# A fused attention and mixture kernel: a quarter of one weight's float64 conversion moves to another stage, with narrower postmix products and a new order where the stages meet

## The chip, the cores and the metric

One core of a Trainium2 chip runs the whole program. The metric is the device time of one execution in microseconds (us). Beside the plain runs there is one profiled execution, whose trace gives every instruction's start and duration. TensorE appears as PE (matmuls) and PEld (its weight loads), VectorE as DVE, ScalarE as ACT, GpSimd as POOL; SPq and ACTq are the instruction queues of SyncE and ScalarE where they issue DMAs.

## The reference

Talking-heads attention over 4 batches, 12 heads, 448 positions and head size 64, then a dense two-layer block, then a soft mixture of 8 experts with 4 slots each. The two weights of the dense block arrive as float64.

```python
scores = scale * np.matmul(q, k.transpose(0, 1, 3, 2))
scores = np.einsum('bhij,hg->bgij', scores, w_pre)
attn = softmax(scores)                       # over j, per mixed head
attn = np.einsum('bhij,hg->bgij', attn, w_post)
x = np.matmul(attn, v)                       # -> (1792, 768)
h = x @ moe_w_in                             # (1792, 2048)
x = (h - np.tanh(h)) @ moe_w_out             # (1792, 768)
logits = x @ phi                             # 32 slots
slot_in = softmax(logits, axis=0).T @ x
slot_out = per expert: relu(slot_in @ w1[e]) @ w2[e]
out = softmax(logits, axis=1) @ slot_out
```

## The kernel before, in words

**Attention** (`talking_heads`) works through 16 chunks of up to 120 query rows. A chunk is cut into slots of up to 10 rows, and slots go in pairs, 92 pairs in all. For a pair, `premix` mixes the heads of the scores on PE (`pm`), DVE takes the row maximum (`mx`), `expo` takes the exponential on ACT (`e`), POOL and DVE make the reciprocal sums and scale the postmix weights (`rv`, `wk`), and two pairs later `postmix` multiplies on PE (`tm`): 32 products of a 64-row by 64-column piece of `e` with 60 columns of `wk`. `gather` copies the result to `aT` on ACT, and `values` multiplies it with v (`vx`). Each piece covers only 56 valid columns (`JH`); the other 8 are zeroes or belong to the next piece, and meet zero rows of v. Scores of the next chunk (`sc`), transposes of q and k, and the re-layout DMA `D<-S` (`regroup`, issued four slots ahead) fill the gaps.

**The float64 conversion** runs beside attention. w_in and w_out are cut into 64 pieces of 128 x 384 elements. A piece is loaded (384 KB), goes through `f64_abs` on ACT, `f64_shift` (two instructions), `f64_head` (one) and `f64_tail` (two) on DVE and `f64_sum` on POOL, and is stored to DRAM (192 KB). A planner in `talking_heads` spreads the pieces evenly over the slots (`due = 6 + i * (NS - D_AHEAD - 17) // len(pieces)`) and picks the calmest slot for each step by its own load counts.

**Stage 1** (`moe_and_slots`) multiplies the tokens in four passes (512, 512, 512 and 256 tokens, `PASS`) with 16 column blocks of w_in; one product is a step `t`, 18 matmuls into a PSUM bank `hp`. Both operands are split into a high and a low part, x by `split_x`, a weight block by `split_w`. In pass 0 each step splits the next weight block (`split_w`, ACT and POOL), saves it to DRAM (`save_w`), gates the last product (five DVE instructions, `gate_first` and `gate_last`), transposes the gated block before that (`turn_g`) and two or three half blocks of w_out (`turn_w`); `turn_bank` hands all transposes two PSUM banks in turn, so that the second `wt` of a step reuses the bank of the first, whose copy DVE makes (L914). Steps 5, 9, 13 and 16 also fold w_out with phi (`fold_first`, `fold_last`). Work is hung on the six parts of a product by `on(c, fn)`. Seven buffers of the expert weights (`mem["ex"]`) are handed to the expert loads from step 17 on; until then 0 to 2 hold w_out blocks and their folds, and 3 to 6 are empty.

**Where the stages meet**, `follow()` is a generator: `next(more)` runs it to its next `yield`. Each engine executes its own instructions strictly in the order written, so what stands behind a waiting instruction waits too.

Of the kernel before, what the change touches and what calls it, by code (L numbers as in the profile page):

```python
# [131 lines left out]
def talking_heads(tc, ident, q, k, v, w_pre, w_post, xd, box, follow):  # L132
# [208 lines left out]
    def recip(s):  # L341
        nc.vector.reciprocal(out=ss_t[s], in_=ss_t[s])  # L342
# [10 lines left out]

    def postmix(s):
        es, wks = e_t.pop(s), wk_t.pop(s)
        xs = [ps.tile([128, 2, NR, NH, IH], FP32, tag="t", name="tm", bufs=2) for _ in range(2)]
        for x in range(2):
            for c in range(NR):
                for i in range(2):
                    for z in range(2):  # L360
                        h = slice(64 * i, 64 * i + 64)
                        j = JP * c + JH * z
                        nc.tensor.matmul(  # L363
                            xs[i][64 * z:64 * z + 64, x, c], lhsT=es[x][h, j:j + 64], rhs=wks[x][h],
                            start=True, stop=True)
        tm_t[s] = xs

# [107 lines left out]
        for lo, hi, hf in ((max(2, t0 - D_AHEAD + 1), t0 + 3, 0), (t0 + 4, start[m - 1] - D_AHEAD - 1, 1)):  # L475
            job(calm("pe", lo, hi), q_half, m, hf, act=0.47, dve=0.53, pe=0.4)
    for m in range(NC):
        step = len(chunks[m + 1][3]) // 3 if m + 1 < NC else 1
        for g in range(3):
            lo = start[m + 1] + T_LAG + 1 + g * step  # L480
            job(calm("pe", lo, lo + step - 1), values, m, g, dve=0.41, pe=2.0)
# [45 lines left out]
    et = [lt.tile([128, SEQ + 64 - JH], FP32, tag=f"e{i}", name="e", bufs=1) for i in range(2 * EB)]  # L527
# [3 lines left out]
    warm = ps.tile([128, 128], FP32, tag="t", name="warm", bufs=2)  # L531

    for p in range(3, NP):
        load_k(0, p)
# [33 lines left out]
    jobs = []  # L568
    more = None
    s = 0  # L570
    while s < NS + T_LAG + 3 or jobs or late:
        live = s < NS
        now[0] = s
        box["both"] = s < NS - D_AHEAD
        if s + D_AHEAD < NS:
            regroup(s + D_AHEAD)
        for f, *a in at.get(("load", s), []):
            f(*a)
        if s % 2 == 0:
            if live:  # L580
                premix(s)
            for f in late:
                f()
            late = []
            if 0 <= s - T_LAG < NS:
                postmix(s - T_LAG)
            if live:
                expo(s)
                guard(s)
        else:  # L590
            if s - 1 < NS:
# [30 lines left out]
    for f in late:  # L622
        f()
    late_stack.close()
    box["go"] = True
    for _ in more:
# [3 lines left out]
def moe_and_slots(tc, ident, xd, wi, wo, wo4, wis, consts, w1, w2, out, box):  # L630
# [161 lines left out]
    def load_x(p):  # L792
        n = PASS[p]
        if p == NPASS - 1:
            xbuf[p] = mem["thp"].tile([128, XW], FP32, tag="x0", name="xc")
            dst = xbuf[p][:, KD * n:2 * KD * n]
        else:
            dst = xbuf[p % 2][1][:, :KD * n]
        nc.sync.dma_start(out=dst.rearrange("p (a s) -> p a s", a=KD), in_=xd[p])

    def split_x(b, c):
        h, l = x_of(b, c, 0), x_of(b, c, 1)
        nc.scalar.activation(out=r32(h), in_=l, func=ACTF.Copy)
        nc.vector.tensor_tensor(out=r32(l), in0=l, in1=h, op=ALU.subtract)

    hps, quads, tok = {}, {}, {}

    def product(t, hooks):
        b, f = divmod(t, NF)
        hp = bank(f"h{t % 3}", [128, PASS[b]], "hp")  # L810
        w = unit(t)
        for c in range(KD):
            for fn in hooks.get(c, []):
                fn()
            m, n = divmod(c, KD // 2)
# [78 lines left out]
    def place(b, k):  # L894
# [2 lines left out]
            return quads["C" if k < 2 else "D"][:, k % 2 * n:(k % 2 + 1) * n]  # L897
        return quads["AECDB"[(b * NQ + k) % 5]]

    def load_o(f):  # L900
        if f < NF:
            nc.sync.dma_start(out=mem["wo"][f % NG], in_=wo[f])

    def turn_w(f, hf):
        x = turn_bank([128, KD // 2, 128], "wt")
        for i in range(KD // 2):
            c = hf * (KD // 2) + i
            nc.tensor.transpose(out=x[:, i, :], in_=mem["wo"][f % NG][:, c * 128:(c + 1) * 128], identity=ident)
# [130 lines left out]
    def step(t):  # L1039
# [345 lines left out]
def fused_kernel(  # L1385
# [40 lines left out]
    def side(hf):  # L1426
# [48 lines left out]
```

## Time and profile before

| | |
|---|---|
| runs (3): median, lowest, highest | 909.75, 909.37, 912.9 us |
| profiled execution: time, span of its instructions | 902.81, 901.1 us |
| busy, share of the span: PE, PEld, DVE, ACT, POOL | 92%, 66%, 62%, 64%, 29% |
| mean granted TensorE clock | 0.983 |
| attention; pass 0 of stage 1; expert tail | to about 471 us; 471 to 560 us; from 800 us |

The busy shares are means over stages that have different limits; what bounds a stage is read in that stage. A wait is idle time of an engine, put down to what ended it.

### The profile page before, as it was taken

To read this page: it belongs to the slowest core of one execution; us is meant where nothing else is said; L and a number is where in the kernel's file an instruction comes from. 1 tells how busy PE (TensorE), PEld (TensorE's weight loads), DVE (VectorE), ACT (ScalarE), POOL (GpSimd) and SP (SyncE) were. 2 spreads that over 40 slices of the span, in tenths; PEclk is the share of its full clock that TensorE was granted. 3 is DMA by queue.
4 is the path that set the end of the run, shared out by engine and by line. 5 is a ranking of instruction groups with operands and counts; after the bars stand their busy time and mean duration, and the time that the engine had idled before them with its cause. 6 is when DMAs were issued, how large, how long until landed. Compare 5 with 4: busy or idle time off the path is not lost.

```text
span 901.1 us, 28664 instructions
## 1 busy us (share of the span) xinstructions
PE 828.2 (92%) x11750; PEld 591.0 (66%) x11750; DVE 558.9 (62%) x1185; ACT 574.3 (64%) x1351; POOL 257.9 (29%) x438
## 2 busy tenths in 40 slices
PE   8878999899989899899889999999999989999985
PEld 6546667566666666566577777767776767865543
DVE  4447868678777678687456666557775776730104
ACT  4757888678877788788656766546654666731013
POOL 6344444444445344445203321000000024600000
PEclk9979999999999999999999999999999999999998
DMA  6988788887888878885758977678754445889998
GB/s 133 229 219 231 224 243 254 233 230 222 237 250 225 232 233 235 247 243 176 235 168 290 316 244 249 231 306 334 277 216 157 159 149 167 317 331 422 424 373 305
DMA packets 145910, 224.53 MB, mean 249 GB/s; under 512 B 60852, under 2 KB 127476, under 8 KB 142196
## 3 DMA queue, kind: packets, MB, share of 16 engines
q1 hardware_dynamic: 142432, 209.83, 73.8%
q10 hardware_dynamic: 3348, 12.87, 3.7%
q8 instruction: 93, 1.52, 0.7%
q14 instruction: 37, 0.30, 0.1%
HBM read 147.96 MB, written 36.18 MB: 204 GB/s over the span
## 4 chain that ended last, share of the span: by engine, by line
PE 63%; DMA 19%; ACT 8%; DVE 6%; issue 3%; SPq 1%; POOL 0%; ACTq 0%; POOLq 0%; DVEq 0%
PE hp L818 25%; DMA D<-S 9%; PE pm L320 6%; PE vx L402 5%; PE sc L286 5%; PE tm L363 4%; ACT e L332 3%; DMA ex<-in_moe_w_dram 3%; PE gt L889 3%; DVE mx L324 3%; DMA xd<-xs 2%; PE lgp L939 2%; ACT S L294 2%; PE so L1301 2%; PE sp L1021 1%
## 5 line engine op out<-in xcount | busy, mean ns | idle before, releaser
L332 ACT ACTIVATE e<-pm,mx 128x448 f32<-128x448 f32 x184 | 115.2, 632 | 84.7 <-DVE mx L324 81.0
L363 PEld LDWEIGHTS tm<-wk,e 64*64 64x64 f32 x5888 | 118.5, 137 | 59.7 <-issue 36.9
L818 PE MATMUL hp<-xa,rg 128*128 128x512 f32 x576 | 152.4, 404 | 0.0
L324 DVE TENSOR_REDUCE mx<-pm 128x1 f32<-128x448 f32 x184 | 106.0, 617 | 65.9 <-PE pm L320 65.5
L363 PE MATMUL tm<-wk,e 64*64 64x60 f32 x5888 | 127.3, 223 | 16.0 <-issue 8.9
L320 PE MATMUL pm<-D,wpre 64*64 64x448 f32 (+2 forms) x736 | 118.5, 568 | 16.7 <-DMA D<-S 13.7
L818 PEld LDWEIGHTS hp<-xa,rg 128*128 128x128 f32 x576 | 102.4, 188 | 28.5 <-issue 10.7
L294 ACT ACTIVATE S<-sc 120x448 f32<-120x448 f32 (+1 forms) x186 | 91.4, 551 | 10.5 <-PE sc L286 5.1
L349 POOL TENSOR_SCALAR wk<-wpost,rv 128x60 f32<-128x60 f32 x184 | 89.3, 507 | 16.1 <-DVE rv L342 11.9
L286 PE MATMUL sc<-khi,qT 64*120 64x448 f32 (+1 forms) x384 | 84.6, 392 | 9.6 <-DVE xs L412 7.2
L780 POOL TENSOR_TENSOR rg<-rg 128x384 fp32r<-128x384 f32 x32 | 32.0, 1014 | 207.1 <-DVE rg L777 191.5
L338 POOL TENSOR_SCALAR rv<-ss 128x2 f32<-128x2 f32 x92 | 26.5, 288 | 219.6 <-ACT e L332 172.7
L402 PE MATMUL vx<-aT,vn 128*64 128x120 f32 (+1 forms) x1536 | 85.7, 266 | 0.3 <-issue 0.2
L849 DVE SCALAR_TENSOR_TENSOR qd<-qd,sq 128x512 f32<-128x512 f32 (+1 forms) x62 | 38.3, 618 | 71.3 <-ACT mk L845 63.3
L402 PEld LDWEIGHTS vx<-aT,vn 128*64 128x64 f32 x1536 | 75.6, 139 | 6.8 <-issue 2.6
L838 ACT ACTIVATE sq<-hp 128x512 f32<-128x512 f32 (+1 forms) x62 | 32.8, 529 | 72.8 <-PE hp L818 72.8
L377 ACT ACTIVATE aT<-tm 128x480 f32<-128x480 f32 x144 | 75.9, 593 | 1.3 <-PE tm L363 1.3
L818 PE MATMUL hp<-xb,rg 128*128 128x512 f32 x288 | 74.7, 404 | 0.0
L70 POOL TENSOR_TENSOR fa<-fa,f 128x384 f32<-128x384 f32 x64 | 67.3, 1052 | 9.1 <-DVE rv L342 3.6
L286 PEld LDWEIGHTS sc<-khi,qT 64*120 64x120 f32 (+1 forms) x384 | 46.7, 174 | 28.2 <-issue 8.1
L320 PEld LDWEIGHTS pm<-D,wpre 64*64 64x64 f32 (+2 forms) x736 | 26.2, 132 | 57.6 <-DMA D<-S 22.7
L818 PEld LDWEIGHTS hp<-xb,rg 128*128 128x128 f32 x288 | 52.0, 188 | 16.6 <-issue 6.3
(185 smaller groups left out, 1392.1 us busy)
## 6 DMA issues: line engine op xcount, KB each, us to landing
ex<-in_moe_w_dram SPq DMA_DIRECT2D x25, 1536.0 KB
D<-S SPq DMA_DIRECT2D x144, 210.0 KB
rg<-wis SPq DMA_DIRECT2D x32, 768.0 KB
f<-in_moe_w_in_dram SPq DMA_DIRECT2D x32, 384.0 KB
f<-in_moe_w_out_dram SPq DMA_DIRECT2D x32, 384.0 KB
wis<-rg ACTq DMA_DIRECT2D x16, 768.0 KB
rg<-wi SPq DMA_DIRECT2D x26, 384.0 KB
wi<-fa SPq DMA_DIRECT2D x32, 192.0 KB
```

Source lines behind the costliest of these rows:

```text
L70: eng.tensor_tensor(out=out, in0=bits(a), in1=bits(p), op=ALU.add)
L286: nc.tensor.matmul(xs[e][0][:ni], lhsT=qT[n][s, l, p, :ni], rhs=kt[s], start=(i == 0), stop=(i == 2))
L294: nc.scalar.activation(out=dst, in_=xs[e][0][:ni], func=ACTF.Copy)
L320: nc.tensor.matmul(xs[x][64 * i:64 * i + 64], lhsT=wpre[k0:k1], rhs=d[i][k0:k1], start=True, stop=True)
L324: nc.vector.tensor_reduce(out=mx[:, x:x + 1], in_=xs[x], op=ALU.max, axis=AX.X, negate=True)
L332: nc.scalar.activation(out=es[x][:, :SEQ], in_=xs[x], func=ACTF.Exp, bias=mx[:, x:x + 1], accum_out=ss[:, x:x + 1])
L349: nc.gpsimd.tensor_scalar(out=wk, in0=wpost, scalar1=rv[:, x:x + 1], scalar2=None, op0=ALU.mult)
L363: nc.tensor.matmul(xs[i][64 * z:64 * z + 64, x, c], lhsT=es[x][h, j:j + 64], rhs=wks[x][h], start=True, stop=True)
L377: nc.scalar.activation(out=out[:, :, c0:c0 + m].rearrange("p a (x i) -> p a x i", x=2), in_=x, func=ACTF.Copy)
L402: nc.tensor.matmul(x[64 * e:64 * e + 64, i, :ni], lhsT=nat_v[b, h // NP][:, h % NP, c, :], rhs=a[:, c, h, :ni], start=(c == 0), stop=(c == ...
L818: nc.tensor.matmul(hp, lhsT=r32(w[:, m, hl, cs]), rhs=r32(x_of(b, c, l)), start=(c == 0 and i == 0), stop=(c == KD - 1 and i == 2))
L849: nc.vector.scalar_tensor_tensor(out=qd, in0=qd, scalar=TG_E, in1=sq, op0=ALU.add, op1=ALU.mult)
```

## The change

1. `LATE = 12`: the eight pieces of w_out from row block 12 on leave the planner's list, which spreads the other 56 over the same slots. In pass 0 of stage 1 they are loaded in steps 2 to 9, get `f64_abs` and `f64_shift` with `f64_head` in steps 4 to 11, `f64_tail` and `f64_sum` in steps 5 to 12, and are stored in steps 6 to 13, in expert buffers 3 to 6. `turn_w` reads them from there, and the four loads of these blocks go.
2. In pass 0, `split_x` for pass 1 subtracts on POOL in place of DVE.
3. The postmix pieces have 56 columns. Their PSUM tiles are two fixed ones that are cleared once.
4. At attention's end the slot loop stops with the last slot, and a short sequence follows: the values of chunk 14 come one pair earlier, `split_w(0)` stands ahead of the x splits, product 0 is run in three parts between the last postmixes, the products of chunk 15's values come together behind it, and the gating of product 0 comes behind them. The first load of x is three DMAs.

```diff
+LATE = 12
@@ postmix
-        xs = [ps.tile([128, 2, NR, NH, IH], FP32, tag="t", name="tm", bufs=2) for _ in range(2)]
+        xs = tms
...
-                            xs[i][64 * z:64 * z + 64, x, c], lhsT=es[x][h, j:j + 64], rhs=wks[x][h],
+                            xs[i][64 * z:64 * z + JH, x, c], lhsT=es[x][h, j:j + JH], rhs=wks[x][h],
@@ planner
-        step = len(chunks[m + 1][3]) // 3 if m + 1 < NC else 1
-        for g in range(3):
+        step = len(chunks[m + 1][3]) // 3 if m + 1 < NC - 1 else 2
+        for g in range(3 if m + 1 < NC else 0):
@@ slot loop
-    while s < NS + T_LAG + 3 or jobs or late:
+    while s < NS:
...
         if s == NS - D_AHEAD:
             early_stack.close()
             more = follow()
-        if more is not None:
             next(more)
         s += 1
-    for f in late:
-        f()
+    for u in range(NS - T_LAG, NS, 2):
+        postmix(u)
+        for f in late:
+            f()
+        late = []
+        next(more)
+        gather(u)
+        next(more)
+    for g in range(3):
+        values(NC - 1, g)()
+    next(more)
@@ late pieces
+    def late_first(i):
+        f64_shift(nc, late_high(i))
+        f64_head(nc, late_high(i), late_high(i), late_raw(i))
+
+    def late_last(i):
+        p = late_raw(i)[:, :, 1]
+        f64_tail(nc, late_high(i), p, late_raw(i))
+        f64_sum(nc.gpsimd, late_half(i), late_high(i), p)
...
@@ step
+        if 0 <= t - 2 < len(late_w):
+            late_load(t - 2)
+        if 0 <= t - 4 < len(late_w):
+            on(3, f64_abs, nc, late_high(t - 4), late_raw(t - 4))
+            on(5, late_first, t - 4)
+        if 0 <= t - 5 < len(late_w):
+            on(5, late_last, t - 5)
+        if 0 <= t - 6 < len(late_w):
+            on(5, late_store, t - 6)
...
-                on(4, split_x, b + 1, f - 8)
+                on(4, split_x, b + 1, f - 8, nc.vector if b else nc.gpsimd)
@@ start of stage 1
-    yield
+    split_w(0, nc.vector)
+    save_w(0)
+    idle = bank("h1", [128, 128], "warm")
+    for _ in range(5):
+        nc.tensor.matmul(idle, lhsT=ident, rhs=ident, start=True, stop=True)
     for i in range(0, KD, 2):
         for c in range(i, i + 2):
             split_x(0, c)
-        if i == 0:
-            split_w(0, nc.vector)
-            save_w(0)
         yield
-    product(0, {})
+        product(0, {}, i, i + 2)
```

PE's order at attention's end, before (the last premix `pm` to the first transposes of step 2; `hp` is a stage-1 product, L402 is `values`):

```order
L320 MATMUL pm<-D,wpre 64x448 x4
L363 MATMUL tm<-wk,e 64x60 x32
L402 MATMUL vx<-aT,vn 64x120 x16
L363 MATMUL tm<-wk,e 64x60 x32
L402 MATMUL vx<-aT,vn 64x120 x16
L818 MATMUL hp<-xa,rg 128x512 x18
L363 MATMUL tm<-wk,e 64x60 x32
L818 MATMUL hp<-xa,rg 128x512 x18
L402 MATMUL vx<-aT,vn 64x88 x48
L818 MATMUL hp<-xa,rg 128x512 x6
```

and of the change (L403 is now `values`, L830 the product, L1177 the five idle products):

```order
L321 MATMUL pm<-D,wpre 64x448 x4
L364 MATMUL tm<-wk,e 56x60 x32
L403 MATMUL vx<-aT,vn 64x120 x16
L364 MATMUL tm<-wk,e 56x60 x32
L1177 MATMUL warm<-ident 128x128 x5
L830 MATMUL hp<-xa,rg 128x512 x6
L364 MATMUL tm<-wk,e 56x60 x32
L830 MATMUL hp<-xa,rg 128x512 x12
L403 MATMUL vx<-aT,vn 64x88 x48
L830 MATMUL hp<-xa,rg 128x512 x24
```

One `vx` has moved ahead of the last `pm`, product 0 is cut around the last `tm`, and product 1 follows the values without a break into step 2.

DVE's order at the same place, before (from the last row maximum; `rg` is `split_w`, `xa` is `split_x`, RECIPROCAL and `xs` belong to attention):

```order
L324 TENSOR_REDUCE mx<-pm 128x1 x2
L804 TENSOR_TENSOR xa<-xa 128x512 x2
L771 TENSOR_TENSOR rg<-rg 128x2x384
L342 RECIPROCAL rv<-rv 128x2
L412 COPY xs<-vx 128x2x12x10
L804 TENSOR_TENSOR xa<-xa 128x512 x4
L771 TENSOR_TENSOR rg<-rg 128x2x384
```

and of the change:

```order
L325 TENSOR_REDUCE mx<-pm 128x1 x2
L413 COPY xs<-vx 128x2x12x10
L343 RECIPROCAL rv<-rv 128x2
L413 COPY xs<-vx 128x2x12x10
L778 TENSOR_TENSOR rg<-rg 128x2x384
L814 TENSOR_TENSOR xa<-xa 128x512 x6
L778 TENSOR_TENSOR rg<-rg 128x2x384
```

The x splits, which wait for a DMA, now stand behind attention's last reciprocal.

DVE's order in one middle step of pass 0, before (gate of the last product, then the first `wt` copy of the next step):

```order
L849 SCALAR_TENSOR_TENSOR qd<-qd,sq 128x512
L850 SCALAR_TENSOR_TENSOR qd<-sq,qd 128x512
L857 TENSOR_TENSOR g<-hp,g 128x512
L862 SCALAR_TENSOR_TENSOR hp<-qd,hp 128x512
L863 COPY_PREDICATED g<-mk,hp 128x512
L914 COPY ex<-wt 128x3x128
```

and of the change (`ex<-ex` are the late pieces' conversions):

```order
L860 SCALAR_TENSOR_TENSOR qd<-qd,sq 128x512
L861 SCALAR_TENSOR_TENSOR qd<-sq,qd 128x512
L868 TENSOR_TENSOR g<-hp,g 128x512
L873 SCALAR_TENSOR_TENSOR hp<-qd,hp 128x512
L874 COPY_PREDICATED g<-mk,hp 128x512
L54 TENSOR_SCALAR ex<-ex 128x384
L55 TENSOR_SCALAR ex<-ex 128x384
L60 SCALAR_TENSOR_TENSOR ex<-ex 128x384
L65 TENSOR_SCALAR ex<-ex 128x384
L66 SCALAR_TENSOR_TENSOR ex<-ex 128x384
L959 COPY ex<-wt 128x3x128
```

Five conversion instructions now stand between the gate and the `wt` copy that frees a transpose bank.

## Rows read from the trace of the kernel before

**Rows 1.** Busy time by stretch: attention, its end, pass 0 (us, instructions, clock, DMA).
```profile
30.00:450.00 420.00, 376.28 (x8508) 269.35 (x8499) 298.99 (x689) 326.69 (x856) 180.95 (x342) 0.98 0.83 231
446.00:471.10 25.10, 20.48 (x353) 17.63 (x344) 11.83 (x21) 14.16 (x33) 1.07 (x3) 0.93 0.56 197
471.10:560.00 88.90, 87.03 (x483) 64.94 (x482) 57.62 (x95) 58.39 (x103) 23.99 (x13) 1.00 0.81 281
```

**Rows 2.** What PE waited for from 30 to 450: total us, times, longest.
```profile
PE pm L320 <- DMA D<-S: 13.4, 12, 3.7
PE tm L363 <- issue: 8.9, 8, 2.8
PE sc L286 <- DVE xs L412: 7.2, 15, 0.8
```

**Rows 3.** PE's timeline in attention: one postmix, what follows (start, us, count).
```profile
328.37 1.11 PE L363 MATMUL tm<-wk,e 64*64 64x60 f32 x64
...
329.41 0.53 PE L265 MATMUL qx<-ident,qn 120*128 120x120 f32 x3
```

**Rows 4.** Weight loads by shape: total busy us, mean ns of one.
```profile
L363 PEld LDWEIGHTS tm<-wk,e 64*64 64x64 f32 x5888 | 118.5, 137 | 59.7 <-issue 36.9 <-POOL wk L349 7.7 <-POOL fa L70 7.1
L286 PEld LDWEIGHTS sc<-khi,qT 64*120 64x120 f32 x288 | 36.1, 181 | 19.8 <-issue 7.1 <-PE tm L363 5.1 <-PE sc L286 1.5
...
L1260 PEld LDWEIGHTS h<-ex,siT 128*32 128x32 f32 x192 | 5.4, 109 | 10.0 <-issue 9.7
```

**Rows 5.** Busy DVE, ACT, POOL on conversion tile f from 30 to 450.
```profile
30.00:450.00 420.00, 101.14 (x192) 37.26 (x64) 67.31 (x64) 0.98 0.83 231
```

**Rows 6.** Three conversion lines: shortest, median and longest ns of 64.
```profile
L53 DVE TENSOR_SCALAR fa<-fa x64: 334/351/1207, 38.0 to 421.8; 128x384 f32<-128x384 f32 x64
...
L54 DVE TENSOR_SCALAR fa<-fa x64: 359/360/1061, 38.4 to 422.2; 128x384 int32<-128x384 int32 x64
...
L59 DVE SCALAR_TENSOR_TENSOR fa<-f,fa x64: 539/549/1256, 39.6 to 423.3; 128x384 int32<-128x384 int32 x64
```

**Rows 7.** Timeline at 386 us: POOL's and DVE's conversion instructions.
```profile
385.80 1.15 POOL L70 TENSOR_TENSOR fa<-fa,f 128x384 f32<-128x384 f32 x1
...
386.12 1.26 DVE L59 SCALAR_TENSOR_TENSOR fa<-f,fa 128x384 int32<-128x384 int32 x1
```

**Rows 8.** Timeline of attention's end, PE, then the x load and its split.
```profile
446.36 1.86 PE L402 MATMUL vx<-aT,vn 128*64 128x120 f32 x32
452.75 2.39 PE L363 MATMUL tm<-wk,e 64*64 64x60 f32 x64 [4.53 <-POOL wk L349]
455.07 2.58 PE L402 MATMUL vx<-aT,vn 128*64 128x120 f32 x32
...
467.28 3.86 PE L402 MATMUL vx<-aT,vn 128*64 128x88 f32 x96
471.07 1.20 PE L818 MATMUL hp<-xa,rg 128*128 128x512 f32 x4
...
440.59 1.65 SPq L799 DMA_DIRECT2D xa<-xd  x1
...
448.67 1.15 ACT L803 ACTIVATE xa<-xa 128x512 fp32r<-128x512 f32 x2 [1.82 <-DMA xa<-xd]
```

**Rows 9.** DVE's timeline over one step of pass 0.
```profile
511.52 0.69 DVE L849 SCALAR_TENSOR_TENSOR qd<-qd,sq 128x512 f32<-128x512 f32 x1 [1.40 <-ACT mk L845]
...
514.80 0.68 DVE L804 TENSOR_TENSOR xb<-xb 128x512 fp32r<-128x512 f32 x1
515.40 0.56 DVE L914 COPY ex<-wt 128x384 f32<-128x384 f32 x1
516.77 0.69 DVE L849 SCALAR_TENSOR_TENSOR qd<-qd,sq 128x512 f32<-128x512 f32 x1 [0.82 <-ACT mk L845]
```

**Rows 10.** PE's timeline in that step: its second `wt`.
```profile
511.04 0.49 PE L908 MATMUL wt<-ident,ex 128*128 128x128 f32 x3
```

**Rows 11.** POOL's timeline in that step: `split_w`, its only work.
```profile
515.75 1.85 POOL L771 TENSOR_TENSOR rg<-rg 128x768 fp32r<-128x768 f32 x1 [3.40 <-PE gt L889]
```

More of the change, by code (lines that the diff above doesn't have):

```diff
@@ L477, in talking_heads @@
     for m in range(NC):
[L478 to L479 removed]
+        step = len(chunks[m + 1][3]) // 3 if m + 1 < NC - 1 else 2
+        for g in range(3 if m + 1 < NC else 0):
             lo = start[m + 1] + T_LAG + 1 + g * step
[L481 removed]
+            job(calm("pe", lo, lo + step - 1) if m + 2 < NC else lo, values, m, g, dve=0.41, pe=2.0)
     pieces = box["early"]
@@ L526, in talking_heads @@
     ds = [lt.tile([128, SEQ], FP32, tag=f"D{i}", name="D", bufs=1) for i in range(DB)]
-    et = [lt.tile([128, SEQ + 64 - JH], FP32, tag=f"e{i}", name="e", bufs=1) for i in range(2 * EB)]
+    et = [lt.tile([128, SEQ], FP32, tag=f"e{i}", name="e", bufs=1) for i in range(2 * EB)]
     vns = [lt.tile([128, NP, NR, HD], FP32, tag=f"vn{i}", name="vn", bufs=1) for i in range(3)]
@@ L530, in talking_heads @@
     wpost = kron("wpost", post_rows, 1.0, False)
-    warm = ps.tile([128, 128], FP32, tag="t", name="warm", bufs=2)
+    warm = ps.tile([128, 128], FP32, tag="p", name="warm")
+    tms = [ps.tile([128, 2, NR, NH, IH], FP32, tag=f"t{i}", name="tm", bufs=1) for i in range(2)]
+    for t in tms:
+        nc.vector.memset(t, 0.0)
     for p in range(3, NP):
@@ L618, in talking_heads @@
             more = follow()
-        if more is not None:
             next(more)
         s += 1
-    for f in late:
-        f()
+    assert not (jobs or halves or [k for k in at if k[1] >= NS])
+    for u in range(NS - T_LAG, NS, 2):
[9 more added lines that the diff above has]
+    next(more)
     late_stack.close()
@@ L798, in load_x, with split_x, product @@
             dst = xbuf[p % 2][1][:, :KD * n]
-        nc.sync.dma_start(out=dst.rearrange("p (a s) -> p a s", a=KD), in_=xd[p])
-    def split_x(b, c):
+        dst = dst.rearrange("p (a s) -> p a s", a=KD)
+        step = KD if p else 2
+        for a in range(0, KD, step):
+            nc.sync.dma_start(out=dst[:, a:a + step], in_=xd[p][:, a:a + step])
+    def split_x(b, c, eng=nc.vector):
         h, l = x_of(b, c, 0), x_of(b, c, 1)
         nc.scalar.activation(out=r32(h), in_=l, func=ACTF.Copy)
-        nc.vector.tensor_tensor(out=r32(l), in0=l, in1=h, op=ALU.subtract)
+        eng.tensor_tensor(out=r32(l), in0=l, in1=h, op=ALU.subtract)
     hps, quads, tok = {}, {}, {}
-    def product(t, hooks):
+    def product(t, hooks, lo=0, hi=KD):
         b, f = divmod(t, NF)
-        hp = bank(f"h{t % 3}", [128, PASS[b]], "hp")
+        if lo == 0:
+            hps[t] = bank(f"h{t % 3}", [128, PASS[b]], "hp")
+        hp = hps[t]
         w = unit(t)
-        for c in range(KD):
+        for c in range(lo, hi):
             for fn in hooks.get(c, []):
@@ L898, in place, with late_raw, late_high, late_half @@
         return quads["AECDB"[(b * NQ + k) % 5]]
+    late_w = box["late"]
+    CV = DM // 2
+    def late_raw(i):
+        return mem["ex"][4 + i // 4].bitcast(I32).rearrange("p (n f w) -> p n f w", n=4, w=2)[:, i % 4]
+    def late_high(i):
+        return mem["ex"][6].bitcast(I32).rearrange("p (n f) -> p n f", f=CV)[:, i]
+    def late_half(i):
+        return mem["ex"][3][:, i * CV:(i + 1) * CV]
+    def late_load(i):
+        f, hf, _ = late_w[i]
+        nc.sync.dma_start(
+            out=late_raw(i).rearrange("p f w -> p (f w)"),
+            in_=box["cv"].w_out[f * 128:(f + 1) * 128, hf * CV:(hf + 1) * CV].bitcast(I32))
+    def late_first(i):
[5 more added lines that the diff above has]
+        f64_sum(nc.gpsimd, late_half(i), late_high(i), p)
+    def late_store(i):
+        f, hf, _ = late_w[i]
+        nc.sync.dma_start(out=wo[f][:, hf * CV:(hf + 1) * CV], in_=late_half(i))
+    def wo_of(f):
+        return mem["wo"][f % NG] if f < LATE else mem["ex"][3][:, (f - LATE) * DM:(f - LATE + 1) * DM]
     def load_o(f):
-        if f < NF:
+        if f < LATE:
             nc.sync.dma_start(out=mem["wo"][f % NG], in_=wo[f])
@@ L1130, in moe_and_slots @@
     load_w(4)
+    mem["g0"] = keep.tile([128, TM], FP32, tag="lp", name="g0")
+    gate_act(0)
     yield
+    split_w(2, nc.vector)
     product(1, {})
     load_w(5)
-    mem["g0"] = keep.tile([128, TM], FP32, tag="lp", name="g0")
-    gate_act(0)
     gate_first(0)
     gate_last(0)
-    yield
-    split_w(2, nc.vector)
     yield
@@ L1439, in fused_kernel @@
         "cv": Conversion(nc, moe_w_in, moe_w_out, wi, wo),
-        "early": order,
+        "early": [j for j in order if not (j[2] and j[0] >= LATE)],
+        "late": [j for j in order if j[2] and j[0] >= LATE],
     }
```

25 lines of the change are left out of this document (9 added, 16 removed).

## The prediction

> **What bounds the kernel now.** I read the busy time by stretch first, then PE's waits in attention, then the timelines of the three places that the change touches. In attention PE is busy 376.3 of 420 us while ACT has 78%, DVE 71% and the DMA engines 0.83 [rows 1]: PE leads, and what can be won is its own work and 43.7 us of waits. Two thirds of these waits have three names: the re-layout `D<-S` 13.4 us in 12 waits, "issue" (nothing that the profile shows) 8.9 us in 8, and DVE's `xs` copy 7.2 us in 15 [rows 2]. At attention's end PE works 20.5 of 25.1 us at a mean granted clock of 0.93, so there is a real hole. In pass 0 of stage 1 PE works 87.0 of 88.9 us: nothing can be won there, and whatever is put there must hide. DVE has 65% and POOL 27% of it [rows 1]. What comes later is not touched; it moves with the end of pass 0.
>
> **The change part by part.** The sum is made against the profiled execution, 902.81 us (span 901.1 and 1.7 around it). The median of the runs shown, 909.75 us, is 0.8% above it; I put the difference on both.
>
> *Postmix of 56 columns.* The 64 instructions of a postmix start at 328.37 and PE goes on at 329.41 [rows 3]: 1.04 us, 16.2 ns each, and since four 64x64 tiles take turns, 65 ns from one load into a tile to the next. A load lasts 109 ns at 32 columns, 137 at 64 and 181 at 120 [rows 4]: (181 - 109) / 88 = 0.82 ns a column. Eight columns fewer are 6.5 ns of the 65 if the load paces the tile, so 64 x 6.5 / 4 = 0.105 us a postmix and 9.7 us for 92. If the 60 moving columns pace it, nothing is won, the lower bound. The 65 ns are nearer to load plus stream (64 x 0.82 = 52 ns for the load alone) than to any stream, so I take the load. But a pair that waits behind its postmix loses the gain: 35 waits in the list of three [rows 2] leave 57 of 92 pairs, so I take 0.6 x 9.7 = **5.8 us** gained, bounds 0 and 9.7. The two clears of the PSUM tiles at the start, and the zeroing of `e` that goes, lie on DVE and POOL before the first postmix and cost nothing; uncovered they would be about 1 us.
>
> *Eight pieces fewer beside attention.* A piece costs DVE 101.1 / 64 = 1.58 us for three instructions on tile `f` [rows 5] and 0.35 + 0.36 us for the two others [rows 6], 2.3 us in all; ACT 0.58 and POOL 1.05 [rows 5]; and 576 KB of DMA. Eight are 18.4 us of DVE, 4.7 of ACT, 8.4 of POOL and 4.7 MB of some 97 MB (231 GB/s for 420 us). None of them leads, so I don't count busy time but waits: an eighth of all 43.7 us of PE's waits is 5.5 us if the conversions caused every one. I take **4 us** gained. Bounds: a loss of 3, since every DMA of attention moves in SP's order and one unlucky re-layout costs up to 3.7 [rows 2], and a gain of 13.4, all waits for `D<-S`.
>
> *Attention's end.* PE stands still for 4.53 us before a postmix at 452.75 [rows 8]. The row names POOL, but POOL's `wk` waited for DVE's reciprocal, which stood behind x splits that waited for a DMA issued at 440.59 and landed at 448.67 [rows 8]. In the new order the reciprocal stands ahead of them. After the hole the postmix took 2.39 us instead of 1.04 and the values 2.58 instead of 1.86 [rows 8, 3]: 2.1 us more, in the stretch whose granted clock is 0.93 [rows 1], that is partly at 1.2 in place of 2.4 GHz. So 6.6 us are there to win. What is late next: five idle products (0.8 us; three transposes take 0.49 [rows 10]), the three parts of product 0 that each wait for their own x splits (I take 0.8), and `turn_g(0)`, whose gate of 3.28 us on DVE (511.52 to 514.80 [rows 9]) now comes behind the values' copies and `split_w(2)` (I take 0.5; 3.3 if wholly uncovered). The values that move ahead of the last `pm` only trade places. **4.5 us** gained, bounds 1.5 and 6.6.
>
> *The pieces in pass 0.* A step without a fold lasts 516.77 - 511.52 = 5.25 us [rows 9]. DVE has 3.28 for the gate and 0.56 for the `wt` copy; the x split at 514.80 leaves. With a piece it is 3.28 + 0.56 + 2.3 = 6.1 us: 0.9 more than the step. The copy stands behind the conversion and frees the bank for the step's second `wt`, at 511.04 where the copy of before could start at once [rows 10, 9]; with 1.4 us of slack at most, PE then waits for DVE. Steps 6, 7, 8, 10 and 11 carry a whole piece and no fold: 5 x 0.9 = 4.5 us. Steps 5 and 9 fold; there DVE catches up, but the copy of the folded weights stands behind the conversion: 0.75 and 0.5. Less the slack of the two groups this is about 5.
>
> POOL gets the sum of a piece (1.05) and an x split (1.3, an estimate between 1.05 for 384 and 1.85 for 768 columns [rows 5, 11]) beside `split_w` (1.85): 4.2 us of a step where it had 1.85. At 386 us DVE's L59 starts 0.3 us into a POOL instruction of 1.15 and lasts 1.26 us, ending 0.4 after it, where its median is 0.55 [rows 7, 6]: DVE stood until POOL was through. In steps 8, 10 and 11 the sum, the weight split and the x split follow each other behind DVE's tail, and DVE's next piece behind them: 4.2 + 2.3 = 6.5 instead of 6.1 us, and the folds' copies are later too. I take **7 us** lost, bounds 3 (slack holds in both groups, folds alone pay) and 11 (half a microsecond more for each piece).
>
> The page "SBUF — State Buffer" of the Trainium skill (section "Who interferes with whom") says that DVE and GpSimd share one pair of ports, that it is an exclusive lock and that the later one blocks for the whole instruction. By that rule pass 0 loses the 7 us and not 5, which would make the sum 2 us better; the row at 386 us agrees with it.
>
> ACT gets 0.58 us in eight steps and has 0.7 to 1.6 idle. DMA gets 3 MB of net loads into 88.9 us at a share of 0.81 [rows 1]; weight loads are issued two steps ahead, so I price it at nothing. If that cover went, a late `split_w` would cost a load, about 1 us a step. A store that waits for POOL holds back what stands behind it on SP, which has the same two steps.
>
> Sum: -5.8 - 4 - 4.5 + 7 = **-7.3 us**, 895.5 us profiled and **902.5 us** for the median.
>
> **The rivals.**
> *Attention gives nothing back.* The postmix is paced by its stream and other waits fill the gaps; for it speaks that DVE's `xs` wait follows `mx`, not the postmix. -4.5 + 7 = +2.5, 912.3 us.
> *The end gives nothing back.* The first w_out blocks or x come late, since PE now runs straight from product 1 into the transposes of w_out and 3.8 us of values no longer lie between. -5.8 - 4 + 7 = -2.8, 907 us. Against it: x comes in three parts, the first of them a third as large.
> *Pass 0 hides the pieces.* If the transposes' banks leave more slack than I count, 2 us are lost: -12.3, 897.5 us.
> *Slower: the DVE-POOL lock decides.* POOL works 4.2 of 5.25 us in these steps. If each of the three lines costs its longest in place of its median [rows 6], 0.86 + 0.70 + 0.71 = 2.3 us a piece, eight cost 18 us more: -14.3 + 7 + 18 = +10.7, 920.5 us. It decides from 18.9 us lost in pass 0, 2.4 a piece. Against it: POOL's sum waits for DVE's tail itself, so the two alternate more than they collide.
>
> **How the numbers follow.** 0.5% is 4.55 us, about what a measurement of this kernel can tell from no change. Forecast 0.45 (898.7 to 905), pass 0 hides them 0.15, nothing from attention 0.20, nothing from the end 0.10, the lock 0.10. Faster is the first two, 0.60; within the bound the next two, 0.30; slower 0.10. The range 894.5 to 912.5 holds all but the lock and the outer end of a pass 0 that hides everything while attention gains its upper bounds.
>
> **What would show it.** The postmix at 0.93 to 0.95 us from its first start to PE's next; `D<-S` and "issue" waits below 22 us; no hole over 1 us from the last `pm` to step 2, at a clock near 1; in pass 0 steps without a fold of 6 to 6.8 us, PE waiting for DVE's `wt` copy in steps 8 and 12 or so, DVE's L54 and L60 of the new file stretched beside POOL. The forecast is wrong if postmix stays at 1.04 us, if PE waits for a DMA in pass 0, or if these steps keep 5.25 us.

## The result and the profile after

Timed against the kernel before, the change takes 898.02 us in place of 909.56 us (medians of four runs each): a ratio of 0.988, interval 0.9835 to 0.9926, which is 10.9 us less. Timed again, with twelve runs against 33, it came to 0.993, 0.9893 to 0.9967, 6.3 us less. The forecast, 902.5 in place of 909.75 us and so 7.3 us less, lies between the two. Single runs of the kernel before lie up to 13 us apart (901.12 to 914.44) even without the slow state that some executions fall into, so the terms have to be read by stage.

I cut each trace at four marks that ACT's timeline shows: A, the first exponential of the last pair; B, the first `sq` of a gate (product 2); C, that of product 15, so that B to C holds 14 gates (the expectations below say 12); D, the last `sq`. All in us, worked out from the starts of those rows:

```
kernel           A     B-A     C-B     D-C   end-D
before      445.50   30.45   84.52  231.26  109.37
after       441.25   24.71   89.37  231.27  111.60
again       448.71   24.70   89.38  229.96  109.05
cols64      443.78   24.78   89.35  230.74  108.25
late16      447.80   25.00   84.95  230.99  109.66
oldend      444.18   31.08   88.93  231.89  109.02
skip24      423.04   24.71   89.37  229.73  108.95
dma24       444.18   24.68   89.34  231.45  109.15
tiny24      433.40   24.67   89.32  229.98  108.93
aftercopy   442.43   24.68   89.11  230.44  112.24
actcopy     443.53   29.24   91.39  230.10  109.14
nodve       449.30   24.69   85.64  231.50  109.47
xdve        446.59   24.71   90.01  231.73  109.16
spread      450.00   24.71   87.47  231.26  109.96
```

Attention's end (B-A) and pass 0 (C-B) repeat within 0.1 us where the kernels differ elsewhere, the ends of actcopy and late16 and the pass 0 of oldend aside: one trace settles them. Attention (A) does not: the ten kernels with 56 loads of pieces beside it stand between 441.25 and 450.00, 445.4 in the mean, and the one trace of before, with 64, stands at 445.50. What moved there is read from timed runs.

The busy time by stretch after the change (columns as in [rows 1]): attention, its end, and pass 0 from B to C; the last line is B to C of the kernel before.

```profile
30.00:450.00 420.00, 374.92 (x8688) 267.09 (x8677) 285.12 (x656) 326.91 (x861) 165.84 (x336) 0.98 0.83 223
439.40:456.00 16.60, 15.90 (x358) 13.06 (x356) 9.15 (x18) 12.01 (x31) 1.93 (x6) 1.00 0.78 260
465.96:555.33 89.37, 83.82 (x461) 61.23 (x461) 68.75 (x124) 61.26 (x109) 37.90 (x27) 1.00 0.86 307
...
475.95:560.47 84.52, 82.65 (x461) 61.29 (x460) 54.39 (x89) 57.23 (x101) 22.14 (x12) 1.00 0.80 279
```

In attention DVE and POOL have less to do than in [rows 1], and PE is no busier. The end has no hole, and its granted clock is 1.00, the level of 2.4 GHz. In pass 0 DVE has risen from 64% to 77%, and PE is idle for 5.6 us in place of 1.9.

PE's timeline at attention's end after the change, against [rows 8], from the premix of the last pair but one; the last two lines are these premixes in the kernel before:

```profile
435.88 0.98 PE L321 MATMUL pm<-D,wpre 64*64 64x448 f32 x8
...
437.63 1.86 PE L403 MATMUL vx<-aT,vn 128*64 128x120 f32 x32
439.42 0.98 PE L321 MATMUL pm<-D,wpre 64*64 64x448 f32 x8
440.22 1.02 PE L364 MATMUL tm<-wk,e 64*56 64x60 f32 x64
441.18 1.86 PE L403 MATMUL vx<-aT,vn 128*64 128x120 f32 x32
443.29 1.42 PE L364 MATMUL tm<-wk,e 64*56 64x60 f32 x64 [0.25 <-ACT aT L382]
444.64 1.38 PE L1177 MATMUL warm<-ident 128*128 128x128 f32 x10
446.42 1.93 PE L830 MATMUL hp<-xa,rg 128*128 128x512 f32 x6 [0.40 <-ACT xa L813]
448.28 1.07 PE L364 MATMUL tm<-wk,e 64*56 64x60 f32 x64
449.27 3.04 PE L830 MATMUL hp<-xa,rg 128*128 128x512 f32 x12
452.24 3.86 PE L403 MATMUL vx<-aT,vn 128*64 128x88 f32 x96
```

```profile
441.06 0.98 PE L320 MATMUL pm<-D,wpre 64*64 64x448 f32 x8
...
443.67 1.58 PE L320 MATMUL pm<-D,wpre 64*64 64x448 f32 x8 [0.69 <-ACT e L332]
```

The 4.53 us before a postmix are now waits of 0.25 and 0.40 us; of the two postmixes that were left behind the hole, the first takes 1.42 us in place of 2.39 and the second 1.07 in place of 1.16 (that one started at 461.88 before). Not all of B-A is gained: the values that moved ahead of the last `pm` (437.63) now stand in front of mark A, and the last two premixes start 3.54 us apart (435.88 to 439.42) where they started 2.61 apart before (441.06 to 443.67). So 0.93 us of the 5.74 only moved.

DVE's timeline over one step of pass 0 after the change, against [rows 9], and POOL's in the same step:

```profile
502.96 0.68 DVE L860 SCALAR_TENSOR_TENSOR qd<-qd,sq 128x512 f32<-128x512 f32 x1
503.68 0.69 DVE L861 SCALAR_TENSOR_TENSOR qd<-sq,qd 128x512 f32<-128x512 f32 x1
504.29 0.68 DVE L868 TENSOR_TENSOR g<-hp,g 128x512 f32<-128x512 f32 x1
504.88 0.69 DVE L873 SCALAR_TENSOR_TENSOR hp<-qd,hp 128x512 f32<-128x512 f32 x1
505.60 0.75 DVE L874 COPY_PREDICATED g<-mk,hp 128x512 f32<-128x512 int32 x1
506.24 0.71 DVE L54 TENSOR_SCALAR ex<-ex 128x384 f32<-128x384 f32 x1
506.99 0.36 DVE L55 TENSOR_SCALAR ex<-ex 128x384 int32<-128x384 int32 x1
507.39 0.56 DVE L60 SCALAR_TENSOR_TENSOR ex<-ex 128x384 int32<-128x384 int32 x1
507.87 0.36 DVE L65 TENSOR_SCALAR ex<-ex 128x384 int32<-128x384 int32 x1
508.26 0.56 DVE L66 SCALAR_TENSOR_TENSOR ex<-ex 128x384 f32<-128x384 uint32 x1
508.73 0.55 DVE L959 COPY ex<-wt 128x384 f32<-128x384 f32 x1
509.20 0.68 DVE L860 SCALAR_TENSOR_TENSOR qd<-qd,sq 128x512 f32<-128x512 f32 x1
```

```profile
505.45 1.29 POOL L814 TENSOR_TENSOR xb<-xb 128x512 fp32r<-128x512 f32 x1
```

No row of DVE's has a wait in brackets: the step is 509.20 - 502.96 = 6.24 us long because DVE's list is. L54, the first conversion instruction, beside POOL's split, takes 0.71 us where the step at 500.38 has 0.34. PE's waits in pass 0 (total us, times, longest):

```profile
PE wt L953 <- DVE ex L959: 3.2, 4, 1.1
PE lgp L984 <- DVE wphi L975: 1.5, 3, 0.7
```

and before the change:

```profile
PE lgp L939 <- DVE wphi L930: 1.1, 3, 0.4
```

All but these 1.1 us are new, and they are the two copies that the forecast named. In attention PE's waits for `D<-S` and "issue" of `tm` come to 16.5 + 5.3 = 21.8 us, just under the 22 that the forecast named as a sign. But those for `D<-S` alone did not fall, 16.5 us in this trace and 14.5 in that of the repeat below against 13.4 [rows 2], so no single trace shows the term of the pieces.

### The profile page after: what moved, and what is told of

It reads as the page before. It is cut to its first block, busy times and chain, and to the rows that moved or that the text cites. A ratio compares the mean times of both kernels' runs of the same rounds, so it can differ in the third digit from the quotient of the medians.

```text
span 898.2 us, 28617 instructions
## 1 busy us (share of the span) xinstructions
PE 823.1 (92%) x11760; PEld 581.5 (65%) x11760; DVE 556.1 (62%) x1181; ACT 573.5 (64%) x1351; POOL 257.0 (29%) x438
## 4 chain that ended last, share of the span: by engine, by line
PE 57%; ACT 13%; DMA 12%; DVE 12%; issue 4%; POOL 1%; SPq 0%; ACTq 0%; POOLq 0%; DVEq 0%
PE hp L830 21%; DMA D<-S 9%; PE pm L321 5%; ACT e L333 5%; PE vx L403 5%; PE sc L287 4%; PE tm L364 4%; DVE mx L325 3%; PE h L1314 3%; ACT S L295 2%; PE so L1355 2%; PE gt L900 2%; PE tz L1334 2%; ACT aT L378 2%; PE lgp L984 2%
## 5 line engine op out<-in xcount | busy, mean ns | idle before, releaser
L830 PE MATMUL hp<-xa,rg 128*128 128x512 f32 x576 | 153.1, 405 | 0.6 <-ACT xa L813 0.4
L364 PEld LDWEIGHTS tm<-wk,e 64*56 64x56 f32 x5888 | 108.5, 130 | 57.0 <-issue 30.7
L321 PE MATMUL pm<-D,wpre 64*64 64x448 f32 (+2 forms) x736 | 113.0, 566 | 19.1 <-DMA D<-S 16.8
L364 PE MATMUL tm<-wk,e 64*56 64x60 f32 x5888 | 117.5, 218 | 10.1 <-issue 5.3
L830 PEld LDWEIGHTS hp<-xa,rg 128*128 128x128 f32 x576 | 102.2, 188 | 30.0 <-issue 10.5
L339 POOL TENSOR_SCALAR rv<-ss 128x2 f32<-128x2 f32 x92 | 24.5, 267 | 229.1 <-ACT e L333 191.0
L350 POOL TENSOR_SCALAR wk<-wpost,rv 128x60 f32<-128x60 f32 x184 | 85.2, 494 | 16.2 <-DVE rv L343 14.5
L403 PE MATMUL vx<-aT,vn 128*64 128x120 f32 (+1 forms) x1536 | 85.3, 263 | 3.7 <-issue 3.2
L403 PEld LDWEIGHTS vx<-aT,vn 128*64 128x64 f32 x1536 | 74.8, 138 | 10.5 <-issue 5.6
L830 PE MATMUL hp<-xb,rg 128*128 128x512 f32 x288 | 74.7, 404 | 0.0
L830 PEld LDWEIGHTS hp<-xb,rg 128*128 128x128 f32 x288 | 52.0, 188 | 16.6 <-issue 6.3
L321 PEld LDWEIGHTS pm<-D,wpre 64*64 64x64 f32 (+2 forms) x736 | 24.8, 132 | 56.8 <-DMA D<-S 22.6
L71 POOL TENSOR_TENSOR fa<-fa,f 128x384 f32<-128x384 f32 x56 | 57.4, 1026 | 7.2 <-DVE rv L343 3.4
```

The source lines that it names most:

```text
L71: eng.tensor_tensor(out=out, in0=bits(a), in1=bits(p), op=ALU.add)
L321: nc.tensor.matmul(xs[x][64 * i:64 * i + 64], lhsT=wpre[k0:k1], rhs=d[i][k0:k1], start=True, stop=True)
L350: nc.gpsimd.tensor_scalar(out=wk, in0=wpost, scalar1=rv[:, x:x + 1], scalar2=None, op0=ALU.mult)
L364: nc.tensor.matmul(xs[i][64 * z:64 * z + JH, x, c], lhsT=es[x][h, j:j + JH], rhs=wks[x][h], start=True, stop=True)
L403: nc.tensor.matmul(x[64 * e:64 * e + 64, i, :ni], lhsT=nat_v[b, h // NP][:, h % NP, c, :], rhs=a[:, c, h, :ni], start=(c == 0), stop=(c == ...
L830: nc.tensor.matmul(hp, lhsT=r32(w[:, m, hl, cs]), rhs=r32(x_of(b, c, l)), start=(c == 0 and i == 0), stop=(c == KD - 1 and i == 2))
```

## The experiments

**The change once more.** No edit.

> The changed kernel itself a second time. In the two traces the last 100 us cost 2.2 us more after the change, of the 5.1 it was ahead at 790 us: 24 h products took 5.35 us at a granted clock of 0.55, in place of 2.78 at 1.00. If that is a matter of the one execution, this trace has the h products at 2.8 us again or the low clock elsewhere, and the ratio to before stays between 0.984 and 0.993. If the change causes it, the low clock stands between 800 and 815 us again.

The ratio was 0.993. Behind D this trace needs 109.05 us, less than before. The 111.60 of the first trace is a matter of that execution. Its rows for 24 `h` products, and then the row of this one:

```profile
809.10 5.35 PE L1314 MATMUL h<-ex,siT 128*32 128x512 f32 x24
...
810.00:815.00 5.00, 4.45 (x24) 0.75 (x16) 0.78 (x4) 0.42 (x1) 0.00 (x0) 0.55 1.00 425
```

```profile
815.19 4.04 PE L1314 MATMUL h<-ex,siT 128*32 128x512 f32 x24
```

Twenty-four such products take 2.78 us at a clock of 1.00. In 11 of the 14 traces one or two of the first groups take longer, by differing amounts; the two longest ends, 111.60 and 112.24 (aftercopy), are the two with a group of 5.35 us.

**Postmix pieces of 64 columns again,** with the zeroing of `e` that they need.

```diff
-   xs[i][64 * z:64 * z + JH, x, c], lhsT=es[x][h, j:j + JH]
+   xs[i][64 * z:64 * z + 64, x, c], lhsT=es[x][h, j:j + 64]
```

> The change with 64-column postmix pieces, as before. The forecast's own term (load-paced postmix, 57 of 92 pairs pass the gain on): 5.8 us slower than the change, ratio to before about 0.994, pairs 14 to 21 of attention with a longer period. Rival, from the two traces: in pairs 14 to 21, 36 to 41 and 58 to 66 the change stands ahead by the same amount from first to last although each postmix is 0.07 us shorter, so the row maximum and the exponentials set the period, and 64 columns cost under 1.5 us: ratio 0.987 to 0.990.

0.9911, 0.9876 to 0.9946: not slower than the change's 0.993. With both intervals the 56 columns can be worth 2.9 us at most in the timed runs, not 5.8. One pair of the change on PE, from premix to premix, and the same pair of this kernel:

```profile
114.83 0.98 PE L321 MATMUL pm<-D,wpre 64*64 64x448 f32 x8
115.63 1.03 PE L364 MATMUL tm<-wk,e 64*56 64x60 f32 x64
116.59 0.46 PE L287 MATMUL sc<-khi,qT 64*120 64x448 f32 x1
117.66 0.43 PE L287 MATMUL sc<-khi,qT 64*120 64x448 f32 x1 [0.61 <-DVE xs L413]
...
119.04 0.98 PE L321 MATMUL pm<-D,wpre 64*64 64x448 f32 x8
```

```profile
117.64 0.98 PE L321 MATMUL pm<-D,wpre 64*64 64x448 f32 x8
118.44 1.11 PE L364 MATMUL tm<-wk,e 64*64 64x60 f32 x64
119.48 0.46 PE L287 MATMUL sc<-khi,qT 64*120 64x448 f32 x1
120.47 0.43 PE L287 MATMUL sc<-khi,qT 64*120 64x448 f32 x1 [0.52 <-DVE xs L413]
...
121.85 0.61 PE L321 MATMUL pm<-D,wpre 64*64 64x448 f32 x4
```

The postmix is 0.96 us long with 56 columns and 1.04 with 64. The 0.08 us come back in the wait for `xs`, 0.61 in place of 0.52 us, and both pairs last 4.21 us. Against the median of seven 56-column kernels, 14 of the 91 intervals between pairs are 0.04 to 0.10 us longer in this trace; they sum to 1.1 us.

**All pieces beside attention again.**

```diff
-LATE = 12
+LATE = 16
```

> The change with all 32 conversion pieces beside attention again, none in pass 0 (the order of attention's end and the 56 columns stay). The forecast's terms: attention loses 4 us, pass 0 gives back 4.9 as the traces show: 1 us faster than the change, ratio 0.987. If the pieces beside attention cost nothing (they only fill gaps): 4.9 us faster, ratio 0.983. If the eight pieces carry the whole gain of attention and delay PE more often: 1 to 3 us slower, ratio 0.99 or more.

0.9968, 0.9934 to 1.0002: 3.4 us slower than the change's 0.993, give or take 4.6. Pass 0 is back at 84.95 us, 4.4 less. So eight pieces cost attention about 8 us, twice the forecast's term, though the interval alone would allow 4.

**The order of before at attention's end.** The loop and the start of stage 1 of before, with 56 columns and late pieces.

```diff
-    while s < NS:
+    while s < NS + T_LAG + 3 or jobs or late:
```

> The change with the order of before at attention's end (56 columns and late pieces stay). Theory: the hole of 4.5 us before the last postmix and the slow clock behind it come back: 5 to 6 us slower than the change, ratio to before about 0.994. Rival: the hole was one late DMA of that one execution and the order alone is worth 2 us or less: ratio 0.990 or less.

0.9981, 0.9945 to 1.0016: 4.6 us slower than the change, give or take 4.7. PE's timeline, then two rows of DVE's:

```profile
451.88 2.23 PE L364 MATMUL tm<-wk,e 64*56 64x60 f32 x64 [5.17 <-ACT aT L382]
454.04 2.81 PE L403 MATMUL vx<-aT,vn 128*64 128x120 f32 x32
...
448.42 1.29 DVE L806 TENSOR_TENSOR xa<-xa 128x512 fp32r<-128x512 f32 x2 [3.81 <-ACT xa L805]
...
450.55 0.16 DVE L343 RECIPROCAL rv<-rv 128x2 f32<-128x2 f32 x1
```

The hole is there again, 5.17 us, and so are the slow rows behind it: B-A is 31.08, and 30.45 before. Neither was a chance of one execution: both traces with the old order have the hole, and in the twelve with the new one PE waits 0.8 us at most for another engine there. The last reciprocal stands behind the x splits, which wait, as the forecast read it. The edit takes back all parts of the new order at once, the three loads of x and the five idle products too; what each part is worth is not shown.

**No w_out piece in attention, two ways.** In skip24 the first edit and the second; in dma24 the first alone, so the loads stay.

```diff
+        if j[2]:
+            return        # absolute, exponent, head, tail
-        ... in_=bits(self.t.pop(j))
+        ... in_=self.fill if o else bits(self.t.pop(j))
```
```diff
+        if o:
+            return        # load
```

> The change with the other 24 w_out pieces left out of attention too: no load, no work on ACT, DVE and POOL, and the store writes a constant, so w_out is wrong. The forecast's term (0.5 us of PE's waits a piece): attention 12 us shorter, ratio to before about 0.979. If the eight pieces that moved were worth 1 us each, as late16 against the repeat of the change says (3.4 us in time and 4.4 us of pass 0): 24 us shorter, ratio 0.966. If the pieces only fill gaps: 3 us at most, ratio 0.989.

> As skip24, but the 24 loads stay and only the work on ACT, DVE and POOL is left out. If a piece costs attention through the DMA queues that the re-layouts share (PE's largest wait there is for the re-layout), this is as slow as the change: ratio 0.990 to 0.993. If it costs through the engines, this is as fast as skip24.

skip24 came to 0.968 (0.963 to 0.9731), dma24 to 0.9906 (0.9868 to 0.9943). The work of 24 pieces on ACT, DVE and POOL is worth nothing that the timing can tell: dma24 is 2.2 us faster than the change, give or take 4.8. Their loads are worth 0.9906 - 0.968 = 2.3%, 20.5 us, 0.85 us each; against the change itself it is 0.993 - 0.968 = 2.5%, 22.6 us, 0.94 us each. Either is good to about a quarter of a microsecond. The stores of 192 KB a piece stay in both kernels, so their price is not shown. PE's wait for the re-layout and the stretch from the first exponential of the fifth pair to that of the last, in dma24, then in skip24:

```profile
PE pm L331 <- DMA D<-S: 16.0, 15, 2.7
...
38.02:444.18 406.16, 363.80 (x8369) 259.31 (x8362) 220.06 (x518) 302.28 (x800) 133.21 (x301) 0.97 0.82 219
```

```profile
PE pm L333 <- DMA D<-S: 8.3, 8, 2.3
...
38.51:423.04 384.53, 347.88 (x8388) 250.06 (x8382) 219.66 (x518) 301.65 (x800) 133.48 (x301) 0.99 0.77 207
```

Without the loads the wait for `D<-S` halves, but that is 7.7 of the 21.6 us between the two stretches. For the same 87 pairs PE is idle 36.7 us in place of 42.4 and busy 347.9 in place of 363.8: most of the difference is longer work of PE, not waits. It is not spread over the loads either. Cut into 22 stretches of four pairs (the last has three), the two traces differ by 20.2 us in the six whose clock was lowered in dma24 (us, granted clock), and by 1.4 us in the other 16 together:

```
pairs        dma24        skip24
5 to 8       25.00 0.89   20.83 0.98
9 to 12      19.56 0.96   19.53 0.94
21 to 24     22.59 0.85   19.91 1.00
33 to 36     24.25 0.93   18.50 1.00
53 to 56     21.26 0.92   19.00 1.00
65 to 68     23.46 0.85   18.10 1.00
other 16    270.04       268.66
```

In pairs 65 to 68 of dma24 PE stands 3.48 us inside a postmix ("issue", nothing that the profile shows), and from 344 to 348 us, right behind it, the granted clock is 0.52. So in these two traces the loads cost time in a few stretches where PE stood and its clock was lowered, and next to nothing elsewhere. How a load brings this about is not shown.

**The same loads, an eighth as large.**

```diff
-    out=r.rearrange("p f w -> p (f w)"),
+    out=r.rearrange("p f w -> p (f w)")[:, :96],
```

> As dma24, but each of the 24 loads fetches an eighth of its bytes (48 KB of 384), at the same place of SP's order. If a piece costs attention the time of its bytes (384 KB at the 425 GB/s of the last 100 us are 0.90 us, 24 of them 22 us), seven eighths come back: 19 us faster than dma24, ratio to before about 0.971. If it costs by standing in SP's order or by the number of transfers: the ratio of dma24, 0.990.

0.9728, 0.9674 to 0.9781, where 0.971 was expected: 16 us against dma24, give or take 6, for seven eighths of the bytes in the same places of SP's order. So it is mostly the bytes, and not the place or the number of transfers. In size the price agrees with the time of 384 KB at the rate of the last stage, where the DMA engines are full:

```profile
815.00:860.00 45.00, 44.52 (x510) 23.22 (x514) 3.15 (x10) 5.12 (x10) 1.75 (x6) 0.96 1.01 413
```

384 KB (393,216 bytes) at 413 GB/s are 0.95 us, and skip24 says 0.85 to 0.94. That the load costs this because the engines move nothing else meanwhile is an inference. By an estimate from attention's own row, 219 GB/s at a share of 0.82, a full share there would move 267 GB/s and 384 KB would take 1.5 us; and the stretches above show the cost in a few places. The trace of tiny24 shows less (A 12 us under the mean of 445.4), but its execution took 888.1 us, the longest of six with a median of 882.65.

**Where the pieces stand in a step of pass 0, and on which engine the copies run.** Three kernels with one profiled execution each, read in C-B alone.

```diff
-            on(5, late_first, t - 4)
+            on(KD, late_first, t - 4)     # aftercopy; late_last, late_store too
```
```diff
-        if hf:
+        if hf or f < 10:                  # actcopy, in turn_w
```
```diff
-    on(4, split_x, b + 1, f - 8, nc.vector if b else nc.gpsimd)
+    on(4, split_x, b + 1, f - 8)          # xdve
```

> The change with a late piece's DVE and POOL work issued at the end of its step, behind the copies out of the transpose bank and of the folded weights. Read in pass 0, from the first to the last of 12 gates, 89.4 us after the change and 84.5 before. If the loss comes from where the pieces stand (PE waits for the bank's copy behind them): 85 to 86 us. If it comes from DVE's work alone, 6.1 us and more in a step of 5.25: 88 to 89.4 us, with PE waiting for the gate instead.

> The change with the transpose bank's copies for w_out blocks 0 to 9 all on ACT; DVE loses 0.55 us a step, ACT gains 0.5. If DVE's total sets the pace (6.24 us a step in the steps at 503 and 525 us): steps of 5.7 us there, pass 0 from 89.4 to about 87 us. If ACT, busy 4.9 to 5.3 us of 6.24, takes its place or PE waits for ACT's copy: 88.5 us or more.

> The change with pass 0's x splits on DVE, as before, in place of POOL. If DVE's total sets the pace, six steps get 0.68 us more and lose the 0.35 us by which DVE's first conversion instruction is stretched beside POOL's x split: 2 us more, 91.4 us from the first to the last of the 12 gates. If the lock between DVE and POOL costs more than the split itself: under 89.4 us.

aftercopy: 89.11 us, 0.26 less. This does not settle whether the place matters, since the edit changes DVE's order only around the copies of the folded weights: in a step without a fold the next step's `wt` copy still stands behind the five instructions, as in the change, and PE's waits for it are the same, 3.2 us in four steps. What speaks against the place is the step of 6.24 us above, in which DVE has no idle time that another order could use. actcopy: 91.39 us, worse; PE now waits for ACT:

```profile
PE wt L953 <- ACT ex L957: 4.6, 7, 0.7
```

xdve: 90.01 us, 0.64 more than the change, between the two expectations. DVE's first conversion instruction beside a split that is now DVE's own:

```profile
511.57 0.68 DVE L814 TENSOR_TENSOR xb<-xb 128x512 fp32r<-128x512 f32 x1
512.16 0.35 DVE L54 TENSOR_SCALAR ex<-ex 128x384 f32<-128x384 f32 x1
```

The stretch beside POOL, 0.35 us of L54, is gone, and the split costs 0.59 more; the step from 508.29 to 514.75 is 6.46 us, 0.22 longer. DVE is held up beside POOL's split, and this costs less than the split itself.

**No DVE work for the late pieces.** `late_first` and `f64_tail` empty.

> The change without the five DVE instructions of each late piece; their loads, ACT's, POOL's instruction and the stores stay, so a quarter of w_out is wrong. Read in pass 0, from the first to the last of 12 gates: 89.4 us after the change, 84.95 with no late piece at all (late16). If DVE's work is the whole loss: 85 us, no wait of PE for the bank's copy. If the loads, POOL or ACT take part: 86 us or more.

85.64 us: 3.7 of the 4.85 us are DVE's. Of the other 1.1 us, 0.49 lie between the first two gates, ahead of any piece. They are in late16 too (0.43), which has no late piece, and not in oldend (0.02), which has all eight: they belong to the new order of attention's end. The last 0.6 us stay with POOL, ACT or the loads.

**Halves dealt out by room.**

```diff
+    for n in range(4, 14):
+        m = 3 if n in folds else 1
+        halves[n] = range(h, h + m) if late_w else []
+        h += m
```

> The change with the 16 halves of the late pieces (three DVE instructions, or two) dealt out by what a step has left: one in each step without a fold from 4 to 12, three in each of the fold steps 5, 9 and 13, behind the copy of the folded weights. If DVE's total in single steps sets the pace, a half of 0.9 to 1.3 us fits the 1.4 us that a step leaves, and three (3.4 us) fit the fold's 2.4 us nearly: 85 to 86.5 us from the first to the last of the 12 gates, 3 to 4 us faster than the change, ratio to before 0.987 to 0.990. If one half too many stands ahead of a copy or a gate everywhere: 88 us or more and the ratio of the change.

87.47 us, 1.9 less than the change, half of what was hoped for: PE still waits for the same copy in five steps, 1.1 us in all. The timed ratio, 0.9954 (0.992 to 0.9988), can't tell this kernel from the change. No version with the right result beat it clearly.

## Why the prediction was right, step by step

**Postmix: -5.8 forecast, -1 measured.** The postmix did get shorter, 1.04 to 0.96 us, nearly the 0.105 worked out. The failed step is "a pair that waits behind its postmix loses the gain: 35 waits in the list of three [rows 2] leave 57 of 92 pairs": only pairs with a listed wait were taken to lose it. The pair above is such a one, the gain comes back in its wait for `xs`. But of the others most lose it too: 14 intervals of 91 pass it on. Where it goes in them is not shown. The 1.1 us are of one trace; the timed runs allow at most 2.9.

**Eight pieces: -4 forecast, about -7 measured** (8 times 0.85 to 0.94 for the loads alone; late16 says 8 give or take 4.6). This is worked out from 24 other pieces, and no timed run settles it for these eight. The failed step is "None of them leads, so I don't count busy time but waits", with an eighth of all waits as the price: most of what the loads cost is not in PE's waits but in the longer time that PE's work takes, 15.9 of 21.6 us in the two traces. The load's bytes set the price (tiny24), at about the rate of full DMA engines; by which path is open. That the pieces' work on DVE, ACT and POOL costs next to nothing there was not foreseen. This term is 3 us too small and the one before 4.7 too large, so that they nearly cancel: that the total came out right is luck to this extent.

**Attention's end: -4.5 forecast, -4.8 measured** (30.45 to 24.71, less the 0.93 us that moved ahead of A), inside its bounds; with the 0.45 us that this order costs between the first two gates it is -4.4. Here the mechanism and the size were right. The allowances came out otherwise one by one: waits of 0.25 and 0.40 us were left around product 0, where 0.8 was allowed; `turn_g(0)` waits 0.76 us for its gate (at 462.52), where 0.5 was; the five idle products take 1.38 us, not 0.8. The values that moved did not "only trade places", they cost the 0.93 us.

**Pass 0: +7 forecast, +4.85 measured.** The mechanism is the one named: DVE's list is longer than the step, and PE waits for the `wt` and `wphi` copies behind it. A step full on DVE lasts 6.24 us, against 6.1 by sum. The loss falls on six of the 13 intervals between gates: 0.46, 0.34, 1.30, 1.00, 0.73 and 1.02 us. The first comes ahead of any piece and belongs to attention's end, as nodve's paragraph says; the steps right behind a fold lose little, since DVE waits 2.38 us for PE there. The other five sum to 4.4, near the 5 of the step count; the 2 us added for POOL were too much. The page "SBUF — State Buffer" of the Trainium skill (section "Who interferes with whom") has DVE and GpSimd share ports by an exclusive lock. The trace agrees that DVE is held up beside POOL, by 0.35 us in three steps and 1.1 us in one (L54 at 521.37, 1.44 us), which is no 2.3 us a piece.

Sum of the measured terms: -1.1 - 7 - 4.8 + 4.85 = -8 us, between the -10.9 and -6.3 timed. **The rivals:** attention gave something (skip24); the end gave its part (oldend); pass 0 did not hide the pieces (4.85, not 2); the lock did not decide.

**Open:** which of POOL, ACT and the loads hold the last 0.6 us of pass 0; by which path a load in attention comes to cost PE time, and what the stores cost; which part of the new order at attention's end does how much; and why attention's length wanders by 9 us between executions of nearly the same program.

## What to carry to other kernels

Where the DMA engines are four fifths busy and the leading engine still waits for transfers, a share of the listed waits can be too low a price for a moved transfer: here its bytes set it, at about the rate of full DMA engines. The same conversion work cost next to nothing in attention, where DVE was 71% busy, and made most of the loss in pass 0, where it filled DVE's step; so price it stage by stage. A saving on the leading engine counts only in those rounds where nothing else stands at the end: compare round by round, between two traces, before multiplying by all of them. Work that is put on a second engine is paid as soon as that engine's list in one step is longer than the step; give it to the steps in which that engine waits (spread: 1.9 us of 4.85 came back in the trace).

## What was not expected of the hardware

A hole of 4.5 to 5.2 us at attention's end was followed both times (before, oldend) by slower products: a postmix of 2.39 or 2.23 us in place of 1.42, and values of 2.58 or 2.81 us in place of 1.86, at a mean granted clock of 0.93 over the stretch before the change [rows 1]. With the hole gone the clock of the stretch was 1.00. No run leaves out the five idle products alone, so what they do for the clock is not shown; in actcopy they stand right behind a stall and take 2.50 us, not 1.38. There PE stood 2.52 us inside the postmix before them for nothing that the profile shows, the clock from 450 to 460 us was 0.76, and the end took 29.24 in place of 24.7 us: a stall of 2.5 us cost 4.5.

```profile
448.78 1.65 PE L364 MATMUL tm<-wk,e 64*56 64x60 f32 x53 [2.52 <-issue]
...
450.00:460.00 10.00, 10.00 (x132) 8.25 (x126) 3.46 (x5) 5.46 (x14) 0.00 (x0) 0.76 0.18 69
```
